# Reordered attention steps in a block-attention and mixture-of-experts kernel

## Chip, cores and metric

The kernel runs on one core of one Trainium2 chip. The metric is device time of one execution, in microseconds (us). Engines are called as the profile calls them: PE (TensorE, matrix products and transposes), PEld (its weight load), DVE (VectorE), ACT (ScalarE), POOL (GpSimd) and SP (SyncE, which issues most DMAs).

## The reference, cut to what matters

Attention runs on 4 batches of 8 heads, 768 positions, 64 columns a head. Each query sees the keys within 15 positions of it, and one maximum over each block of 32 keys; the values that go with the maxima are block means. The rows of the result are then routed to one of 4 groups and one of 4 experts in it, and each token passes through that expert's two matrices.

```python
k_sum = k.reshape(B, H, nb, block, D).max(axis=3)
v_sum = v.reshape(B, H, nb, block, D).mean(axis=3)
scores_l = scale * np.matmul(q, k.transpose(0, 1, 3, 2))      # kept where |i - j| < 16
scores_s = scale * np.einsum('bhsd,bhnd->bhsn', q, k_sum) + np.log(block)
scores_all = np.concatenate([scores_l_m, scores_s], axis=-1)
a = np.exp(scores_all - np.max(scores_all, axis=-1, keepdims=True))
a = a / (np.sum(a, axis=-1, keepdims=True) + 1e-09)
attn_out = np.matmul(a, np.concatenate([v, v_sum], axis=2))
...
h = np.maximum(xg[mask_e] @ w1[g, e], 0.0)
out[tok_idx] = combined[:, None] * (h @ w2[g, e])
```

## The kernel before

**Tiling.** Attention takes two heads at a time: 16 head pairs (`order`, idx 0 to 15), each in three groups (g 0, 1, 2), so 48 groups n = 3·idx + g. A group holds 256 queries of both heads. What follows attention (routing tables, one expert's four blocks, pairs of blocks, single blocks) isn't touched by the change.

**Order of work.** The order in which each engine gets its instructions is written out by hand: `PLAN` (L49) lists the steps of a group for g = 0, 1, 2, and `START` (L52) replaces it for the first groups. The loop at the end of `attention` walks through that list. Every engine works through its own queue in this order, and waits by semaphore for what others make. The steps are:

- s, `scores` (L780): eight score products of 64 by 64 parts of the PE array into two of the three banks `ps_s`; then DVE makes four passes (L795) that add the mask and take a minimum (`ss`, `nm`).
- e, `exps` (L801): four exponentials on ACT (L804) into `pr`.
- t, `transpose_p` (L807): four PE transposes of `pr` of two groups before, into a bank `ps_tr`; ACT copies them to `ptS` (L812).
- v, `values` (L815): eight products of 64 array columns into the one bank `ps_av`, for the group of three before; DVE takes a reciprocal (L826) and multiplies (L827) into `xt`.
- p0, p1 (`put_k`, L760): four transposes of the next pair's keys `kn` for one head each, into `ps_tr`, and two copies (L764) from there into `kw`, j = 0 and j = 1. p2, p3 (`put_q`): the same for the queries, copied by ACT (L758) into `qt`.
- p4 (L769 to L778): on DVE, two copies of neighbouring keys within `kw` (L772, L773), the maxima over 32 keys (L775, `ks`), and their broadcast into the last columns of `kw` (L778). All score products of the next pair read `kw`.
- m0, `means` part 0 (L721): 24 products of 32 array columns with `stair`, and DVE's copy `vp` (L731). m1: two more products, DVE's copy `vr` (L735), and POOL's copies of it into `va` (L738).
- l0, l1 (`logits`): four and two transposes of `xt`, copied to `xT` (L848). l2: eight products of 32 array columns with `wcat`. l3: every fourth pair, two DVE operations (L864, L865) that fill `lg`.

The PE array is thus divided in four ways: whole (all transposes), in 64 by 64 (s), in 64 columns (v), in 32 columns (m0, m1, l2).

**Banks.** `ps_tr` and `ps_s` have three banks each, `ps_av` and `ps_lg` one. `Banks.next` hands them out in turn, so the fourth transpose block waits for the copies of the first.

**Routing.** The tokens' routing is some hundred small DVE operations. `advance(n)` puts the next n of them into DVE's queue at places set by `OPS` (L61): two after v, two within p4 between the maxima and their broadcast, one after the minimum passes of s. Routing work for the three first batches is queued at groups 17, 29 and 41 (`ROUTE_AT`).

**DMAs.** SP issues them in the order of the code. `load_qk` brings keys and queries of a pair (two DMAs of 384 KB), `load_vw` its values in six (L647). The first group of a pair issues values for idx + 2 and then keys and queries for idx + 3. `keep_warm` (L659) puts zero products on PE whose result nobody reads.

Of the kernel before, what the change touches and what calls it, by code (L numbers as in the profile page):

```python
# [20 lines left out]
P = 128  # L21
# [7 lines left out]
NBLK = S // BLOCK  # L29
QT = 64  # L30
RUN = 8
NQT = S // QT

KW = QT + 2 * PAD
NC = KW + NBLK
# [10 lines left out]
EPS = 1e-9  # L46
NEG = -1.0e9

PLAN = [["s", "p0", "l1", "t", "v", "p1", "e", "p4"],  # L49
        ["s", "p2", "t", "v", "m1", "l2", "e"],  # L50
        ["s", "p3", "l3", "t", "v", "l0", "m0", "e"]]
START = [["s", "e"], ["s", "m0", "e"], ["s", "w", "t", "m1", "p0", "p1", "e", "p4", "p2", "p3"],  # L52
         ["t", "v", "s", "n0", "p0", "p1", "e", "p4"]]
LAG = {"l0": 1, "l1": 2, "l2": 2, "l3": 2}

T_LAG, V_LAG = 2, 3
# [1 line left out]
ACT_K1 = range(10, B * NP)  # L58

ROUTE_AT = (17, 29, 41)  # L60
OPS = dict(m=2, k=2, s=(1, 1, 1))  # L61


W1_AT = 34
# [25 lines left out]
class Clock:  # L90

    pe, dve = float("-inf"), 0.0
    step = 0
# [496 lines left out]
def attention(tc, q, k, v, w_group, w_expert, ident, x_dram, ps, router, hook):  # L590
    nc = tc.nc
# [4 lines left out]
    def advance(ops):  # L596

        for _ in range(ops):
            r = next(work[0], work) if work else "wait"
            if r is work:  # L600
                work.pop(0)
            elif r == "wait":
                break
# [6 lines left out]
    V = nc.vector  # L610
    T = router.T
    ps_tr, ps_s, ps_av, ps_lg = ps["tr"], ps["s"], ps["av"], ps["lg"]
    lg = router.lg

    with ExitStack() as st, ExitStack() as nat_st:
# [6 lines left out]
        order = [(b, a) for b in range(B) for a in range(NP)]  # L622
# [16 lines left out]
        def load_vw(idx):  # L639

            b, a = order[idx]
            va = va_ring[idx % NVA][:, :, :, 0:D]
            src = v[b, 2 * a:2 * a + 2]
            for rows, key, t0, t1 in ((slice(0, QT), 0, 0, NQT), (slice(QT, QT + PAD), QT - PAD, 1, NQT),
                                      (slice(QT + PAD, KW), QT, 0, NQT - 1)):
                for h in range(2):
                    nc.sync.dma_start(out=va[rows, t0:t1, h],  # L647
                                      in_=bass.AP(src.tensor, src.offset + (h * S + key) * D,
                                                  [[D, rows.stop - rows.start], [QT * D, t1 - t0], [1, D]]))
# [9 lines left out]
        def keep_warm(n):  # L659
            t = ps_lg.next()  # L660
            for _ in range(n):
                nc.tensor.matmul(out=t, lhsT=zero, rhs=zero[:, None, :].broadcast_to([P, 4, P]), start=True, stop=True)  # L662
# [37 lines left out]
        m = mask[:, 0, 0:KW]  # L700
# [20 lines left out]
        def means(idx, part):  # L721

            va = va_ring[idx % NVA]
            t = ps_tr.next()
            if part == 0:
                for i in range(NQT):
                    j = i % 4
                    T.matmul(out=t[32 * j:32 * j + 32, 0:P], lhsT=stair[:, NBLK - 2 - 2 * i:NBLK + 30 - 2 * i],
                             rhs=va[0:KW, i, :, 0:D], start=(i < 4), stop=(i >= NQT - 4), skip_group_check=True)
                vps[idx] = sm.tile([P, P], F32, name="vp", bufs=2)  # L730
                V.tensor_copy(out=vps[idx], in_=t[:, 0:P])  # L731
            else:
                T.matmul(out=t[KW:NR, 0:P], lhsT=same, rhs=vps.pop(idx), start=True, stop=True)
                vr = wk.tile([NR, 1, 2, D], F32, name="vr")
                V.tensor_copy(out=vr[KW:NR].rearrange("p a h d -> p (a h d)"), in_=t[KW:NR, 0:P])  # L735
                n = 2
                for i in range(0, NQT, n):
                    nc.gpsimd.tensor_copy(out=va[KW:NR, i:i + n, :, 0:D], in_=vr[KW:NR].broadcast_to([NBLK + 1, n, 2, D]))  # L738


        def prep(idx, part):
            qn, kn = qk[idx]
            qb, kw = qts[idx % 2], kws[idx % 2]

            def tr(src, h):

                t = ps_tr.next()
                n = S // RUN
                for i in range(4):
                    T.transpose(out=t[:, i * n:(i + 1) * n], in_=src[:, h, 2 * i:2 * i + 2].rearrange("p j d -> p (j d)"),  # L750
                                identity=ident[0:n, 0:n])
                return [t[64 * j:64 * j + 64, 0:4 * n].rearrange("p (i t r) -> p i t r", i=4, t=NQT) for j in range(2)]

            def put_q(h):
                rows = slice(64 * h, 64 * h + 64)
                out = qb[rows].rearrange("p t (i j) r -> p j t i r", j=2)
                for j, tv in enumerate(tr(qn, h)):
                    nc.scalar.activation(out=out[:, j], in_=tv.rearrange("p i t r -> p t i r"), func=AF.Copy, scale=-1.0 / 8.0)  # L758

            def put_k(h):  # L760
                rows = slice(64 * h, 64 * h + 64)
                out = kw[rows, :, 0:QT].rearrange("p t (r i j) -> p j t r i", i=4, j=2)
                for j, tv in enumerate(tr(kn, h)):
                    (nc.scalar.copy if j == 0 or h and idx in ACT_K1 else V.tensor_copy)(  # L764
                        out=out[:, j], in_=tv.rearrange("p i t r -> p t r i"))
            if part < 2:
                put_k(part)
            elif part < 4:
                put_q(part - 2)  # L769
            else:  # L770

                V.tensor_copy(out=kw[:, 1:NQT, before], in_=kw[:, 0:NQT - 1, QT - PAD:QT])  # L772
                V.tensor_copy(out=kw[:, 0:NQT - 1, behind], in_=kw[:, 1:NQT, 0:PAD])  # L773
                ks = sm.tile([P, NBLK], F32, name="ks")
                V.reduce_max(out=ks, axis=AX.X,  # L775
                             in_=kw[:, :, 0:QT].rearrange("p t (a k) -> p t a k", k=BLOCK))
                advance(OPS["k"])
                V.tensor_copy(out=kw[:, :, KW:NC], in_=ks[:, None, :].broadcast_to([P, NQT, NBLK]))  # L778

        def scores(n):  # L780

# [10 lines left out]
            for h in range(2):  # L792
                for j in range(2):
# [3 lines left out]
                                           accum_out=nm[:, u:u + 1])  # L797
            advance(OPS["s"][g])
            return ss, nm
# [71 lines left out]
        NG = 3 * len(order)  # L871
        prs, pts = {}, {}

        for part in (0, 1, 4, 2, 3):
            prep(0, part)
        keep_warm(9)
        for t in prr:
# [9 lines left out]
        for n in range(NG + 3):  # L887
            idx, g = n // 3, n % 3
            if n < NG:
                b, a = order[idx]  # L890
                xs[b] = x_ring[b % 2]
            for step in START[n] if n < len(START) else PLAN[g]:
                if step == "s" and n < NG:
                    sps = scores(n)
                elif step == "e" and n < NG:
                    prs[n] = exps(n, *sps)
                elif step == "t" and 0 <= n - T_LAG < NG:
                    pts[n - T_LAG] = transpose_p(prs.pop(n - T_LAG))
                elif step == "v" and 0 <= n - V_LAG < NG:
                    values((n - V_LAG) // 3, (n - V_LAG) % 3, pts.pop(n - V_LAG))  # L900
                elif step[0] == "p" and n < NG and idx + 1 < len(order):
                    prep(idx + 1, int(step[1]))
                elif step[0] == "m" and n < NG:
                    j = idx + (step == "m0" and n > 2)
                    if (j > 0 or n < 3) and j < len(order):
                        means(j, int(step[1]))
                elif step == "w":
                    keep_warm(4)
                elif step == "n0":
                    means(1, 0)  # L910
                elif step[0] == "l" and 0 <= idx - LAG[step] < len(order):
                    logits(idx - LAG[step], int(step[1]))
            if n == 0:
                router.consts()
            elif n == 4:
                router.compared()
            if n in ROUTE_AT:
                b1 = ROUTE_AT.index(n)
                work.append(router.route(b1 * TB, (b1 + 1) * TB))
                if b1 == 1:  # L920
                    work.append(router.first_blocks())
            if n == NG - 4:
                nat_st.close()
            if n < NG:
                if g == 0 and idx + 2 < len(order):
                    load_vw(idx + 2)
                if g == 0 and idx < len(order) - 3:
                    qk[idx + 3] = load_qk(idx + 3)
            if g == 1 and stores:
                store()  # L930
            while stores and n == NG - 5:
                store()
            clock.step += 1
            hook(n, need, advance, w1_first)
# [514 lines left out]
```

## Time and profile before

| | us |
|---|---|
| median of 3 runs | 516.33 |
| lowest and highest run | 514.16, 518.73 |
| profiled execution, its time | 515.85 |
| profiled execution, span from first to last instruction | 514.2 |

1.65 us of the profiled execution lie outside its span. Attention runs from the first score products at 9.42 us to about 179 us; the rest belongs to the experts. Times below count from the start of the span. In the timeline a row is a run of like instructions: start, length, engine, line, what it writes and reads, count, and in brackets the idle time before it with what ended it. The length of a PE row includes the pipeline's end, which overlaps the next row, so the step from one start to the next is the measure.

### The profile page before, as it was taken

Reading aid. Unit: us, or ns where it says so; the run is one execution under the profiler, and the core shown is the slowest. Engines: PE = TensorE matmul, PEld = TensorE weight load, DVE = VectorE, ACT = ScalarE, POOL = GpSimd, SP = SyncE. Lnnn points to the kernel's source line nnn. Section 1 sums busy time; section 2 is a strip of 40 time slices with the busy share of each in tenths; the row PEclk is TensorE's granted clock in tenths of the full one; section 3 lists DMA queues with packets and bytes.
Section 4 is the critical chain, followed back from the end, with each engine's and each line's share of the span. In section 5 each row is a group of like instructions: output and inputs, shape, how many; then the busy total and the mean of one; then the engine's idle time right before and its main releaser. Section 6 shows DMA issues by size and latency. Waiting matters only on the chain.

```text
span 514.2 us, 13346 instructions
## 1 busy us (share of the span) xinstructions
PE 492.2 (96%) x4974; PEld 415.5 (81%) x4974; DVE 356.6 (69%) x1084; ACT 317.8 (62%) x597; POOL 120.9 (24%) x205
## 2 busy tenths in 40 slices
PE   8999999999999899999999999999999999999994
PEld 4677767776777698979898989898898989897773
DVE  6687899888977978878755647483836556473773
ACT  5699888888988643216644556473645546474682
POOL 6122112211312600037020203022121202022332
PEclk9799999999999899999999999999999999999998
DMA  9999676879646820069997665665566756754891
GB/s 179 176 181 198 130 168 189 180 155 195 173 113 224 281 90 22 28 220 354 409 403 273 238 229 211 247 225 190 205 211 239 263 212 222 258 191 137 300 359 42
DMA packets 75316, 106.94 MB, mean 208 GB/s; under 512 B 40286, under 2 KB 40366, under 8 KB 75232
## 3 DMA queue, kind: packets, MB, share of 16 engines
q1 hardware_dynamic: 69184, 86.78, 58.5%
q0 software_dynamic: 6048, 19.12, 10.4%
q8 instruction: 43, 0.70, 0.6%
q14 instruction: 41, 0.34, 0.2%
HBM read 97.49 MB, written 13.24 MB: 215 GB/s over the span
## 4 chain that ended last, share of the span: by engine, by line
PE 49%; issue 19%; DMA 12%; DVE 11%; ACT 3%; POOL 3%; POOLq 1%; DVEq 0%; ACTq 0%
PE ps_s L122 26%; DMA out_dram<-y,t_unit_scatter 12%; PE ps_tr L122 12%; PE ps_av L122 10%; DVE ss L795 3%; DVE ks L775 2%; DVE kw L764 1%; ACT kw L764 1%; PE ps_lg L122 1%; POOL ohr L1042 1%; ACT qt L758 1%; PE ps_lg L662 1%; POOLq L1185 1%; ACT pr L804 1%; DVE kw L778 1%
## 5 line engine op out<-in xcount | busy, mean ns | idle before, releaser
L122 DVE TENSOR_TENSOR w2l<-w2r,w2h 128x1024 fp32r<-128x1024 f32 x52 | 63.4, 1225 | 77.1 <-ACT w2h L1035 76.6
L122 PE MATMUL ps_s<-xT,w1h 128*128 128x256 f32 x448 | 83.5, 284 | 0.0
L122 PEld LDWEIGHTS ps_s<-xT,w1h 128*128 128x128 f32 x448 | 70.7, 192 | 1.0 <-issue 0.7
L1082 POOL DMA_INDIRECT out_dram<-y,t_unit_scatter x24 | 25.7, 1069 | 190.9 <-ACT y L1077 97.7
L738 POOL COPY va<-vr 25x256 f32<-25x256 f32 x96 | 35.9, 418 | 118.8 <-DVE vr L735 118.8
L122 PE MATMUL ps_s<-xT,w1l 128*128 128x256 f32 x224 | 63.4, 283 | 0.0
L122 DVE TENSOR_TENSOR w1l<-w1r,w1h 128x1024 fp32r<-128x1024 f32 x52 | 60.4, 1219 | 3.6 <-ACT w1h L1035 3.6
L804 ACT ACTIVATE pr<-ss,nm 128x120 f32<-128x120 f32 x192 | 60.1, 387 | 3.3 <-DVE nm L795 2.9
L1120 ACT ACTIVATE hTh<-ps_s 128x512 fp32r<-128x512 f32 x48 | 28.7, 598 | 53.9 <-PE ps_s L122 31.9
L122 PE MATMUL ps_s<-ohr,w1h 128*128 128x256 f32 x320 | 58.9, 282 | 0.0
L1035 ACT CAST w2h<-w2r 128x1024 fp32r<-128x1024 f32 x52 | 53.8, 1041 | 1.5 <-DVE lg L865 0.9
L1035 ACT CAST w1h<-w1r 128x1024 fp32r<-128x1024 f32 x52 | 50.7, 1051 | 0.4 <-DMA w1r<-in_moe_w_dram 0.4
L122 PEld LDWEIGHTS ps_s<-ohr,w1h 128*128 128x128 f32 x320 | 49.8, 188 | 0.2
L122 DVE SCALAR_TENSOR_TENSOR hTl<-ps_s,hTh 128x512 fp32r<-128x512 f32 x48 | 33.2, 691 | 24.2 <-ACT hTh L1120 21.5
L795 DVE CUSTOM_DVE_ANT_0 ss<-mask,ps_s 128x120 f32<-128x120 f32 x192 | 42.1, 275 | 6.1 <-PE ps_s L122 4.6
L122 PE MATMUL ps_s<-ohr,w1l 128*128 128x256 f32 x160 | 45.0, 281 | 0.0
L122 PEld LDWEIGHTS ps_s<-xT,w1l 128*128 128x128 f32 x224 | 42.9, 192 | 0.3
L122 PE MATMUL ps_s<-kw,qt 64*64 64x120 f32 x768 | 37.5, 282 | 5.7 <-DVE nm L795 4.6
L122 PE MATMUL ps_s<-w2h,hTh 128*128 128x512 f32 x104 | 41.6, 400 | 0.0
L122 PE MATMUL ps_av<-w2h,hTh 128*128 128x512 f32 x104 | 41.6, 400 | 0.0
L122 PE MATMUL ps_av<-w2l,hTh 128*128 128x512 f32 x104 | 41.1, 395 | 0.0
L122 PE MATMUL ps_s<-w2h,hTl 128*128 128x512 f32 x104 | 41.1, 395 | 0.0
(275 smaller groups left out, 1010.6 us busy)
## 6 DMA issues: line engine op xcount, KB each, us to landing
w1r<-in_moe_w_dram SPq DMA_DIRECT2D x30, 1024.0 KB, 8.4
w2r<-in_moe_w_dram SPq DMA_DIRECT2D x28, 1024.0 KB, 5.6
kn<-in_k_dram SPq DMA_DIRECT2D x16, 384.0 KB, 4.5
qn<-in_q_dram SPq DMA_DIRECT2D x16, 384.0 KB, 5.4
va<-in_v_dram SPq DMA_DIRECT2D x32, 192.0 KB, 5.0
x_dram<-xt SPq DMA_DIRECT2D x12, 512.0 KB, 5.4
w2r<-in_moe_w_dram POOLq DMA_DIRECT2D x4, 1024.0 KB
va<-in_v_dram SPq DMA_DIRECT2D x64, 44.0 KB, 4.6
```

The costliest lines, as they stand in the source:

```text
L122: return f(*args, **kw)
L662: nc.tensor.matmul(out=t, lhsT=zero, rhs=zero[:, None, :].broadcast_to([P, 4, P]), start=True, stop=True)
L738: nc.gpsimd.tensor_copy(out=va[KW:NR, i:i + n, :, 0:D], in_=vr[KW:NR].broadcast_to([NBLK + 1, n, 2, D]))
L758: nc.scalar.activation(out=out[:, j], in_=tv.rearrange("p i t r -> p t i r"), func=AF.Copy, scale=-1.0 / 8.0)
L764: (nc.scalar.copy if j == 0 or h and idx in ACT_K1 else V.tensor_copy)(out=out[:, j], in_=tv.rearrange("p i t r -> p t r i"))
L775: V.reduce_max(out=ks, axis=AX.X, in_=kw[:, :, 0:QT].rearrange("p t (a k) -> p t a k", k=BLOCK))
L778: V.tensor_copy(out=kw[:, :, KW:NC], in_=ks[:, None, :].broadcast_to([P, NQT, NBLK]))
L795: V.tensor_tensor_reduce(out=ss[:, u], in0=mask[:, 1 if t == 0 else 2 if t == NQT - 2 else 0], in1=sp[h][:, j], scale=1.0, scalar=3.4e38, ...
L804: nc.scalar.activation(out=pr[:, i, 0:NC], in_=sp[:, i], func=AF.Exp, bias=nm[:, i:i + 1], scale=-1.0)
L1035: self.nc.scalar.copy(out=h, in_=src)
L1082: self.nc.gpsimd.indirect_dma_start(out=self.out, out_offset=bass.IndirectOffsetOnAxis(ap=self.tabs[name, "scatter"][0:y.shape[0], col:col ...
L1120: nc.scalar.activation(out=th[:, js], in_=hp, func=AF.Relu)
```

## The change

The lists of steps are written anew. Products with 32 array columns (m0, l2, m1) now stand together in g = 1, and all full-array transposes of a group stand in one run behind the score products. p4 is split: the copies of neighbours stay p4 and move to g = 1, the maxima and their broadcast become p5 in g = 2. m0 writes a bank of `ps_s` in place of `ps_tr`. Of the key copies, both of the first head go to ACT; of the second head j = 0 goes to ACT from idx 10 on (as `ACT_K1` says), j = 1 to DVE. Routing advances by three behind the broadcast (two between maxima and broadcast before), and not at all behind the minimum passes of g = 2. Values of pair 3 are issued at group 0, right behind those of pair 2, and so ahead of keys and queries of pair 3. The opening gets two and three more zero products (w2, w3) and its lists reach to group 5.

```diff
-PLAN = [["s", "p0", "l1", "t", "v", "p1", "e", "p4"],
-        ["s", "p2", "t", "v", "m1", "l2", "e"],
-        ["s", "p3", "l3", "t", "v", "l0", "m0", "e"]]
-START = [["s", "e"], ["s", "m0", "e"], ["s", "w", "t", "m1", "p0", "p1", "e", "p4", "p2", "p3"],
-         ["t", "v", "s", "n0", "p0", "p1", "e", "p4"]]
+PLAN = [["s", "t", "l1", "p0", "p1", "v", "e"],
+        ["s", "t", "p4", "p2", "v", "m0", "l2", "m1", "e"],
+        ["s", "p5", "t", "p3", "l0", "l3", "v", "e"]]
+START = [["s", "e"], ["s", "m0", "e"], ["s", "w4", "t", "m1", "p0", "p1", "e", "p4", "p5", "p2", "w2", "p3"],
+         ["t", "v", "w3", "s", "n0", "p0", "p1", "e"], ["s", "t", "p4", "p2", "v", "m1", "e"],
+         ["s", "p5", "t", "p3", "v", "l0", "m0", "e"]]
...
-OPS = dict(m=2, k=2, s=(1, 1, 1))
+OPS = dict(m=2, k=3, s=(1, 1, 0))
...
-            t = ps_tr.next()
+            t = (ps_tr if part else ps_s).next()
...
-                    (nc.scalar.copy if j == 0 or h and idx in ACT_K1 else V.tensor_copy)(
+                    (nc.scalar.copy if h == 0 or j == 0 and idx in ACT_K1 else V.tensor_copy)(
...
-            else:
+            elif part == 4:
                 V.tensor_copy(out=kw[:, 1:NQT, before], in_=kw[:, 0:NQT - 1, QT - PAD:QT])
                 V.tensor_copy(out=kw[:, 0:NQT - 1, behind], in_=kw[:, 1:NQT, 0:PAD])
+            else:
                 ks = sm.tile([P, NBLK], F32, name="ks")
                 V.reduce_max(out=ks, axis=AX.X,
                              in_=kw[:, :, 0:QT].rearrange("p t (a k) -> p t a k", k=BLOCK))
+                V.tensor_copy(out=kw[:, :, KW:NC], in_=ks[:, None, :].broadcast_to([P, NQT, NBLK]))
                 advance(OPS["k"])
-                V.tensor_copy(out=kw[:, :, KW:NC], in_=ks[:, None, :].broadcast_to([P, NQT, NBLK]))
...
-        for part in (0, 1, 4, 2, 3):
+        for part in (0, 1, 4, 5, 2, 3):
             prep(0, part)
...
-                elif step == "w":
-                    keep_warm(4)
+                elif step[0] == "w":
+                    keep_warm(int(step[1]))
...
-                if g == 0 and idx + 2 < len(order):
+                if g == 0 and idx != 1 and idx + 2 < len(order):
                     load_vw(idx + 2)
+                    if idx == 0:
+                        load_vw(3)
```

## Rows read from the trace of the kernel before

**Rows 1.** Windows, head pairs 1, 4 and 11, edges at their first score products
```profile
core 0: us, PE busy (x) PEld busy (x) DVE busy (x) ACT busy (x) POOL busy (x), PEclk, DMA share, GB/s
18.70:30.34 11.64, 11.48 (x159) 8.76 (x159) 7.83 (x40) 8.26 (x20) 2.25 (x6) 0.71 1.26 189
...
49.82:59.55 9.73, 9.50 (x168) 7.43 (x164) 8.02 (x39) 8.73 (x23) 2.13 (x6) 1.00 0.66 142
...
121.11:131.76 10.65, 10.15 (x175) 7.77 (x171) 9.13 (x50) 9.32 (x24) 2.61 (x8) 1.00 0.90 184
```

**Rows 2.** Timeline of head pair 4, PE's blocks
```profile
47.82 0.69 PE L122 MATMUL ps_av<-va,ptS 121*64 121x65 f32 x16
...
48.44 0.66 PE L122 MATMUL ps_tr<-ident,xt 128*128 128x128 f32 x4
...
49.02 0.86 PE L122 MATMUL ps_tr<-va,stair 96*32 96x128 f32 x24
...
49.82 0.64 PE L122 MATMUL ps_s<-kw,qt 64*64 64x120 f32 x16
...
50.39 0.55 PE L122 MATMUL ps_tr<-ident,kn 96*128 96x96 f32 x4
...
50.77 0.38 PE L122 MATMUL ps_tr<-ident,xt 128*128 128x128 f32 x2
...
51.00 0.60 PE L122 MATMUL ps_tr<-ident,pr 128*121 128x128 f32 x4
...
55.40 0.42 PE L122 MATMUL ps_s<-kw,qt 64*64 64x120 f32 x2
...
56.62 0.55 PE L122 MATMUL ps_tr<-ident,qn 96*128 96x96 f32 x4
```

**Rows 3.** Timeline of head pair 4, DVE's operations
```profile
50.02 0.29 DVE L731 COPY vp<-ps_tr 128x128 f32<-128x128 f32 x1 [0.83 <-ACT pr L804]
...
50.51 0.28 DVE L795 CUSTOM_DVE_ANT_0 ss<-mask,ps_s 128x120 f32<-128x120 f32 x1 [0.20 <-PE ps_s L122]
...
53.26 0.56 DVE L764 COPY kw<-ps_tr 64x384 f32<-64x384 f32 x1 [0.19 <-ACT kw L764]
...
54.20 0.94 DVE L775 TENSOR_REDUCE ks<-kw 128x24 f32<-128x768 f32 x1
...
55.17 0.31 DVE L778 COPY kw<-ks 128x288 f32<-128x288 f32 x1
...
55.51 0.28 DVE L795 CUSTOM_DVE_ANT_0 ss<-mask,ps_s 128x120 f32<-128x120 f32 x1
...
56.31 0.18 DVE L826 RECIPROCAL rs<-ps_av 128x4 f32<-128x4 f32 x1
```

**Rows 4.** DVE's waits, 69.30 to 164.05 us: total us, times, longest
```profile
DVE kw L772 <- ACT kw L764: 2.6, 6, 0.7
DVE vp L731 <- ACT xT L848: 2.2, 3, 1.1
DVE rs L826 <- PE ps_av L122: 1.9, 4, 1.1
...
DVE vp L731 <- ACT pr L804: 1.2, 2, 0.8
```

**Rows 5.** Costliest groups of the page: the exponentials on ACT
```profile
L804 ACT ACTIVATE pr<-ss,nm 128x120 f32<-128x120 f32 x192 | 60.1, 387 | 3.3 <-DVE nm L795 2.9
```

**Rows 6.** Timeline of the opening: zero products, DMA issues on SP, key transposes
```profile
12.69 1.04 PE L662 MATMUL ps_lg<-zero 128*128 128x512 bf16 x4
...
22.51 0.38 SPq L633 DMA_DIRECT2D kn<-in_k_dram  x1
...
23.74 5.85 SPq L647 DMA_DIRECT2D va<-in_v_dram  x6
...
30.91 0.55 PE L122 MATMUL ps_tr<-ident,kn 96*128 96x96 f32 x4
```

**Rows 7.** DMA issues of the page: count, KB, median us to landing
```profile
kn<-in_k_dram SPq DMA_DIRECT2D x16, 384.0 KB, 4.5
```

## The prediction, made before the changed kernel ran

> **What bounds the kernel now.** I read the page first: PE is busy nearly all the span, which for pipelined products says little. So I cut attention, the only part that the change touches, into windows by head pair [rows 1]. Pair 4 takes 9.73 us, with PE busy 9.50, ACT 8.73, DVE 8.02, at full granted clock; pairs 2 to 5 are alike. Pair 11 stands for pairs 6 to 14, where routing work is under way: 10.65 us, DVE busy 9.13 although one key copy of it has gone to ACT. The nine pairs from 69.30 to 164.05 us take 94.75 us, 10.53 each. Pair 1, in the opening, takes 11.64 us at a mean granted clock of 0.71, that is partly at 1.2 in place of 2.4 GHz; against 9.73 this is 1.9 us.
>
> Next the timeline of pair 4 [rows 2], start to start. Score products take 0.57 us (49.82 to 50.39). The score products at 55.40 take 1.22 until the next block at 56.62, 0.65 more. DVE's rows [rows 3] say why: it goes from the key copy (53.26) through the maxima (54.20) and the broadcast (55.17) to the minimum passes at 55.51 without a pause, and the second score bank is free only when the passes of the group before are done. So in pairs 2 to 5 PE sets the pace, with one stall of 0.65 us behind DVE.
>
> DVE itself waits in every pair [rows 3]: 0.83 us ahead of the copy vp, 0.20 ahead of the minimum passes, 0.19 ahead of a key copy. The wait of vp is labelled with ACT, but what vp reads is the block of 24 products that PE began at 49.02 [rows 2]. From 69.30 to 164.05 us [rows 4] DVE waits 2.6 us for ACT ahead of L772, 2.2 + 1.2 ahead of vp, 1.9 for the value products: 7.9 of 94.75 us. With routing in its queue DVE is close to being the bound there, and its waits are what can be gained.
>
> **The change, part by part.**
>
> *Fewer changes of array division.* Counting through the lists, a pair before goes whole, 64 by 64, whole, 64 columns and so on in 13 changes; after, in 10. What one costs: four transposes between two changes take 0.58 us (48.44 to 49.02), two in the middle of a run 0.23 (50.77 to 51.00), so four would take 0.46; the difference, 0.12, is what a run pays for its changes [rows 2]. Bounds are 0, where PE waits anyway, and 0.2. Three fewer are 0.36 us of PE time a pair. Here a rule of the Trainium skill speaks against the gain: the page TensorEngine Tiling (Array Packing), section PSUM Bottleneck, says in substance that packing speeds up PE but not the emptying of PSUM, which may then become the bound, and advises to use both ScalarE and VectorE for it. By that rule alone the 0.36 would be worth nothing. The traces bear it out in part: ACT and DVE, which empty the banks, are busy 8.73 and 8.02 of 9.73 us [rows 1], so little room is left below 9 us. It is the third of the cases below.
>
> *p4 split and moved, routing behind the broadcast.* DVE now does neighbours in g = 1 and maxima and broadcast in g = 2, behind that group's minimum passes. The stall of 0.65 goes, since between two groups' minimum passes there is never more than one of these. What comes in its place: the next pair's score products need the broadcast, made in the group just before them. From the start of g = 2's score products: 0.69 until DVE's first pass (49.82 to 50.51), 0.80 for four passes (55.51 to 56.31), 0.97 for the maxima (54.20 to 55.17), 0.34 for the broadcast (to 55.51): 2.80 us [rows 2, 3]. PE's own work in g = 2 is 0.57 for scores, 0.46 for t, 0.38 for p3 (as 50.39 to 50.77), 0.58 for l0, 0.62 for v (47.82 to 48.44): 2.61 [rows 2]. So PE waits 0.2 us a pair if DVE is not late, and one for one more if it is. Moving advance behind the broadcast takes two operations out of this path; the count of routing operations a pair stays 11 (six behind v, three, two).
>
> *Full-array run t, l1, p0, p1.* p1 is the fourth block in three banks, so it waits for the copy ptS of t. That copy stands in ACT's queue behind the exponentials of the group before, four of 387 ns [rows 5]. The wait is between 0 and 1.5 us; I take 0.4, since PE has scores, t, l1 and p0 to do first.
>
> *Key copies by head.* The count on each engine stays two and two (three and one from idx 10). Now no half is split over both, except from idx 10 on. Before, DVE's copy started only when ACT's was done [rows 3], and p4 right behind it waited for ACT [rows 4]; after, p4 runs a group later, when these copies are old. m0's bank from ps_s lets its products go without waiting for a transposed bank, but it takes score banks: g = 2's scores now need all minimum passes of g = 1. PE has 3 us of work in between, so I set this at nothing; if DVE is later than that, it is part of the fourth case.
>
> So pairs 2 to 5: 0.36 + 0.65 gained, 0.2 + 0.4 lost, 0.4 each, 1.6 us together (9.3 a pair). Pairs 6 to 14: DVE's list is as long as before, so only its waits count. Those for ACT and for m0, 6.0 us, lose their cause; I give back 1.2 for new ones: 4.8 us. Bounds are 0 and the whole 7.9.
>
> *Fourth values sooner.* On SP, keys and queries of pair 3 go behind six more DMAs. Before, keys were issued at 22.51 and those six took 5.85 us of SP (from 23.74) [rows 6]. After, keys leave at about 28.4 and, with the median landing of 4.5 us [rows 7], arrive by 32.9. The transposes that need them began at 30.91 [rows 6]. So p0 of group 6 can be up to 2.0 us late; what follows it in its group is shorter than before by t and l1, 0.5 + 0.2 us [rows 2]. That is a loss of up to 1.3 us, or of nothing if the keys come 2 us sooner than their median.
>
> *Zero products.* Five more, 0.26 us each by 12.69's row [rows 6], 1.3 us, stand where PE waits for ACT and DVE in the opening and are hidden; uncovered they cost that. They may keep the clock at 2.4 GHz through pair 1, worth up to 1.9 us. But whatever pair 1 gains, p0 of group 6 then waits for its keys. So I set the opening at 0, from 1.9 gained to 2.6 lost. Such a wait can itself bring the clock down a little later.
>
> *End of attention and experts.* Pair 15 prepares no next pair, and the experts' code is the same: 0.
>
> Sum: 515.85 - 1.6 - 4.8 = 509.45 for an execution like the profiled one. This was 0.48 below the median of 516.33, so I predict 509.9.
>
> **The rivals.**
>
> *All engines reach their floors.* Pairs 2 to 5 fall to PE's 9.73 - 0.65 - 0.36 = 8.7 (4.0 us), all of DVE's 7.9 go, and the opening keeps the 1.9: 515.85 - 13.8 + 0.48 = 502.5. For it: DVE's floor in pair 4 is 9.73 - 1.22 = 8.5. Against: three engines would have to be full at once.
>
> *Emptying sets the pace.* DVE and ACT have the same work to do, and while routing runs nothing is gained: only the 1.6 of pairs 2 to 5 stays, 515.85 - 1.6 + 0.48 = 514.7. The rule of the Trainium skill named above would have it so. For it: the same instructions on both; against: the waits in [rows 4] are of order, not of work.
>
> *The broadcast comes too late: slower.* While routing runs, six operations of a pair's 11 lie on DVE between g = 0's start and g = 2's minimum passes. Pair 11's DVE is 1.1 us busier than pair 4's, and with the 0.56 of the copy that left, routing is 1.7 us a pair [rows 1, 3]; six of eleven are 0.9. If DVE reaches the passes of g = 2 that much late, PE waits 0.2 + 0.9 + 0.4 where it saved 1.0: 0.5 lost a pair, 4.5 in nine, less 1.6: 515.85 + 2.9 + 0.48 = 519.2; with all 1.7 late, 526. It decides from a lateness of 0.4. For it: s is at the head of every group. Against: in these pairs DVE, not PE, is nearly the bound, and a PE wait is then free.
>
> **How the numbers follow.** Forecast 0.52, floors 0.13, emptying 0.23, broadcast 0.12. The forecast's own range is 506.5 to 513, by the bounds of its 4.8 and of the opening. Leaving out half of the floors' case below and most of the last above, the range is 503.5 to 519. One per cent, about what a measurement of this kernel can tell from no change, is 5.2 us: faster means under 511.2, slower over 521.5. Three quarters of the forecast and all of the floors' case are faster, 0.52; the last case's upper half and some opening trouble are slower, 0.09; the rest, 0.39, is the same.
>
> **What would show it.** Pairs 2 to 5 at 9.2 to 9.4 us; score products at the head of a pair waiting 0.2 to 0.4 us for the broadcast; the waits of key copies and L772 for ACT gone from DVE's list; DVE busy over 9.3 of some 10.0 us in pairs 6 to 14; a PE wait of 1 to 3 us for kn at group 6, near 29 to 32 us. I'd be wrong if pairs 6 to 14 stay at 10.5 (emptying, or the broadcast), if PE's wait for the broadcast is over 1 us, or if the opening moves by more than 2 us.

## The result and the profile after

| | before | after |
|---|---|---|
| median, us (13 runs each, beside each other) | 515.80 | 520.96 |
| lowest and highest run, us | 513.86, 518.95 | 516.45, 522.52 |
| ratio of after to before, 95% interval | | 1.0089 [1.0068, 1.0111] |
| profiled execution: its time, span, us | 515.85, 514.2 | 517.72, 516.0 |

The changed kernel is slower by 0.9%, 4.6 us by the ratio, where 6.4 us less were forecast, and lies beyond the top of the range. The profiled execution of it is one of its three quickest, so its trace shows less of the loss than the median: 1.9 us.

From the page of the changed kernel, its span, busy times and granted clock in 40 slices:

```profile
span 516.0 us, 13360 instructions
...
PE 483.7 (94%) x4979; PEld 413.1 (80%) x4979; DVE 353.9 (69%) x1084; ACT 314.9 (61%) x597; POOL 120.5 (23%) x205
...
PEclk9999999999999999999999999999999999999998
```

This execution ran attention at full clock throughout, where the one before had 1.2 GHz in part of pair 1 [rows 1]. Up to the first score products of pair 15 the two are level, 164.09 us after and 164.05 before, with some 1.3 us of before's spent at the lower clock in pair 1 (b0, below). The 1.8 us between their spans lie behind that, where the code is the same: 0.3 up to the experts' first product, 0.5 up to PE's last, 1.0 behind it. So the loss of the medians can't be read from this one pair of traces; what they do show is where the forecast gains went. Windows of the changed kernel by head pair (1, 2, 4, then 6 to 14, then 11), columns as in [rows 1]:

```profile
18.97:27.89 8.92, 8.64 (x160) 6.62 (x159) 7.22 (x39) 7.13 (x18) 2.26 (x6) 1.00 1.08 162
27.89:40.23 12.34, 9.49 (x168) 7.72 (x164) 7.86 (x39) 9.18 (x24) 2.14 (x6) 1.00 1.12 210
49.76:59.58 9.82, 9.12 (x164) 7.47 (x164) 7.75 (x40) 8.42 (x23) 2.14 (x6) 1.00 0.81 140
69.39:164.09 94.70, 83.63 (x1505) 68.17 (x1505) 80.79 (x427) 82.34 (x215) 19.26 (x54) 1.00 0.78 179
120.67:131.40 10.73, 9.35 (x172) 7.61 (x172) 8.57 (x50) 8.82 (x24) 2.14 (x6) 1.00 0.85 179
```

Against [rows 1]: pair 1 went from 11.64 to 8.92 us, pair 4 from 9.73 to 9.82, pairs 6 to 14 from 94.75 to 94.70, pair 11 from 10.65 to 10.73. Pair 2, 9.73 before, takes 12.34. In pair 4 PE is busy 0.38 us less than before and the pair is longer: PE's work did shrink, and waiting took its place. In pairs 6 to 14 PE is busy 5.1 us less (88.72 to 83.63), DVE the same (81.20 to 80.79), and nothing came of it. By the starts of score products the nine pairs fall in two parts: pairs 6 to 8 take 30.75 us for 31.66 before, pairs 9 to 14 take 63.95 for 63.09. What the first three gained, 0.9, the last six lost.

**Where pair 4 waits.** Timeline of the changed kernel, pair 4, answering to [rows 2] and [rows 3]:

```profile
49.76 0.70 PE L123 MATMUL ps_s<-kw,qt 64*64 64x120 f32 x16 [0.29 <-DVE kw L779]
...
51.14 0.49 PE L123 MATMUL ps_tr<-ident,kn 96*128 96x96 f32 x4
...
51.43 0.57 ACT L814 COPY ptS<-ps_tr 121x512 f32<-121x512 f32 x1
...
52.05 0.36 PEld L123 LDWEIGHTS ps_tr<-ident,kn 96*128 96x128 f32 x4 [0.60 <-ACT ptS L814]
52.05 0.55 PE L123 MATMUL ps_tr<-ident,kn 96*128 96x96 f32 x4 [0.42 <-ACT ptS L814]
...
52.71 1.13 DVE L765 COPY kw<-ps_tr 64x384 f32<-64x384 f32 x2 [0.87 <-PE ps_tr L123]
...
58.00 0.59 ACT L814 COPY ptS<-ps_tr 121x512 f32<-121x512 f32 x1 [0.94 <-PE ps_tr L123]
...
58.61 0.69 PE L123 MATMUL ps_av<-va,ptS 121*64 121x65 f32 x16
```

The reader is to see two stalls of PE. p1 (52.05) can't start until ACT has emptied t's bank into `ptS`; PE's weight loads stand idle 0.60 us for it, PE 0.42, and DVE then waits 0.87 for the second head's transposes. And the score products at the head of a pair wait for the broadcast (49.76); from 58.61, where v begins, to the next pair's score products at 59.58 it is 0.97 us, where v alone took 0.62 [rows 2]. That is 0.35. ACT is late with `ptS` at one end of the pair and itself waits 0.94 for PE at the other (58.00): a loop, not an engine that is full.

**Where pairs 6 to 14 wait.** Waits from 69.39 to 164.09 us in the changed kernel: us in total, times, longest; first DVE's, then PE's:

```profile
DVE kw L765 <- ACT kw L765: 7.8, 6, 1.9
...
PE ps_s L123 <- DVE kw L779: 4.8, 8, 1.0
```

The waits of [rows 4] are gone, and one new line of DVE's, 7.8 us, is as long as all of them together (7.9). All of it lies behind 100.14 us, where the keys of idx 10 and later are prepared and the second head's two copies are split: j = 0 on ACT, j = 1 on DVE, and DVE's follows ACT's, which is the third of three copies in a row on ACT.

**The opening.** Timeline of the changed kernel, PE and SP, answering to [rows 6]:

```profile
14.72 12.57 SPq L648 DMA_DIRECT2D va<-in_v_dram  x12
27.39 0.38 SPq L634 DMA_DIRECT2D kn<-in_k_dram  x1
...
29.27 0.38 PE L123 MATMUL ps_tr<-ident,xt 128*128 128x128 f32 x2
31.93 0.85 PE L123 MATMUL ps_tr<-ident,kn 96*128 96x96 f32 x8 [2.27 <-DMA kn<-in_k_dram]
```

Keys of pair 3 left SP at 27.39 in place of 22.51, and PE waited 2.27 us for them in pair 2.

### The profile page after: what moved, and what is told of

Read it like the earlier page. It is cut to its first block, busy times and chain, and to the rows that moved or that the text cites. A ratio compares the mean times of both kernels' runs of the same rounds, so it can differ in the third digit from the quotient of the medians.

```text
span 516.0 us, 13360 instructions
## 1 busy us (share of the span) xinstructions
PE 483.7 (94%) x4979; PEld 413.1 (80%) x4979; DVE 353.9 (69%) x1084; ACT 314.9 (61%) x597; POOL 120.5 (23%) x205
## 5 line engine op out<-in xcount | busy, mean ns | idle before, releaser
L1086 POOL DMA_INDIRECT out_dram<-y,t_unit_scatter x24 | 27.0, 1126 | 190.0 <-ACT y L1081 97.6
L739 POOL COPY va<-vr 25x256 f32<-25x256 f32 x96 | 34.4, 403 | 118.7 <-DVE vr L736 109.2
L123 PE MATMUL ps_s<-w2l,hTh 128*128 128x512 f32 x104 | 41.1, 395 | 0.0
```

The source lines that it names most:

```text
L123: return f(*args, **kw)
L1086: self.nc.gpsimd.indirect_dma_start(out=self.out, out_offset=bass.IndirectOffsetOnAxis(ap=self.tabs[name, "scatter"][0:y.shape[0], col:col ...
```

## Experiments

One table for all runs, read from the starts of score products in each trace: time from the first of all score products to the first of pair 3 (the opening), the length of pair 4, and that of pairs 6 to 14; in us.

| run | opening | pair 4 | pairs 6 to 14 | profiled execution |
|---|---|---|---|---|
| before | 30.65 | 9.73 | 94.75 | 515.85 |
| before again (b0) | 29.30 | 9.73 | 94.76 | 514.66 |
| after | 30.81 | 9.82 | 94.70 | 517.72 |
| after again (a1) | 29.72 | 9.81 | 94.61 | 519.10 |
| a2 values late | 29.81 | 9.81 | 94.60 | 517.53 |
| a3 copies | 34.02 | 9.82 | 91.27 | 520.29 |
| a4 maxima early | 30.86 | 9.82 | 95.85 | 520.79 |
| a5 p1 behind v | 30.14 | 9.33 | 90.51 | 516.38 |
| a6 m0 back | 31.41 | 9.30 | 92.76 | 515.16 |
| a7 no zeros | 31.78 | 9.81 | 94.61 | 517.49 |
| b1 values alone | 32.72 | 9.73 | 94.75 | 517.47 |
| c1 = a2 + a5 | 30.36 | 9.33 | 90.51 | 511.67 |
| c2 = a2 + a5 + a6 | 27.89 | 9.05 | 89.40 | 508.43 |

The two columns on the right of the opening repeat to 0.1 us between runs of like code; the opening does not. So each stage is judged by its own column, and the opening by the medians as well.

**a1: the changed kernel again**, for runs beside those of a2 to a4.

> The changed kernel, unaltered, for the spread of its runs and a second trace. Theory C (clock and late keys): the wait for the keys of pair 3 in group 6, 2.27 us in the first trace, lowers the granted clock soon after in most runs; runs with mean clock 0.994 or more take 516 to 518 us, runs near 0.985 take 521 to 522.5, and a trace with the lower clock has a stretch at 1.2 GHz between 30 and 45 us. Theory W (waits moved) expects pairs 3 to 5 near 9.8 us in any trace, and the difference between runs elsewhere than in the opening.

520.71 us against 517.58 for before, ratio 1.0079 [1.0047, 1.0110]. The loss holds.

**a2: fourth values at their old place.**

```diff
-                if g == 0 and idx != 1 and idx + 2 < len(order):
+                if g == 0 and idx + 2 < len(order):
                     load_vw(idx + 2)
-                    if idx == 0:
-                        load_vw(3)
```

> Values of pair 3 issued at group 3 again, behind keys and queries of pair 3. Theory C: the wait for keys in group 6 (2.27 us) goes, means of pair 3 may wait about 1 us for their values, the clock no longer falls there, and the time is 3 to 5 us lower than the changed kernel's. Theory W: the opening gains at most 1 to 2 us and the pairs from 3 on stay at 9.5 to 9.8 us.

517.84 us, ratio to before 1.0010 [0.9988, 1.0032], where the changed kernel had 1.0079 beside it. This edit alone takes away the loss, some 3.6 us by the ratios and 2.9 by the medians; pair 4 and pairs 6 to 14 don't move. The values have their own deadline, though: m0 stands in g = 1 since the change, and PE waits 0.49 us for them in a2's pair 2 and 1.39 in that of c1 below. In c2, with m0 back in g = 2, there is no such wait. From the windows of a2, pair 2:

```profile
28.71:39.42 10.71, 9.52 (x168) 7.74 (x165) 7.91 (x40) 8.63 (x23) 2.13 (x6) 1.00 1.30 180
```

**b1: the fourth values sooner in the kernel before, nothing else** (the same lines, the other way round).

> The kernel before with the values of pair 3 sent at group 0, alone. Theory C: p0 of group 6 waits for its keys 1 to 2 us, a fall of the clock near 32 us follows in a part of the runs, and the time is 1 to 3 us above the kernel before. If the order of these DMAs doesn't matter: the same time within 0.5 us.

517.98 us, ratio 1.0075 [1.0043, 1.0107]. This is the mirror of a2: one edit to the kernel before makes nearly the whole loss (3.9 us by the ratio, 2.9 by the medians). Timeline of b1's PE, and its windows of pairs 1 and 2:

```profile
31.76 0.52 PE L122 MATMUL ps_tr<-ident,kn 96*128 96x96 f32 x4 [1.92 <-DMA kn<-in_k_dram]
```
```profile
18.70:29.20 10.50, 9.09 (x159) 6.78 (x159) 7.79 (x40) 8.24 (x20) 2.21 (x6) 1.00 1.15 173
29.20:42.13 12.93, 11.01 (x169) 8.65 (x165) 8.11 (x39) 8.72 (x23) 2.17 (x7) 0.87 1.10 213
```

The same wait of PE for the same keys, and behind it a granted clock of 0.87 over pair 2: part of that pair ran at 1.2 GHz. Pair 2 took 12.93 us, 3.2 more than before's 9.73.

**a3: from idx 10 on the first head's copies are split, not the second's.**

```diff
-(nc.scalar.copy if h == 0 or j == 0 and idx in ACT_K1 else V.tensor_copy)(
+(nc.scalar.copy if (h == 1 or j == 0 if idx in ACT_K1 else h == 0) else V.tensor_copy)(
```

(Three copies stay on ACT from idx 10 on, but DVE's one is now of the first head, whose transposes are p0's and early.)

> From pair 10 on, the key copies go as before (first head: ACT and DVE, second head: both ACT); earlier pairs as in the change. Theory W: DVE's wait for ACT ahead of its key copy, 7.8 us in 6 waits in pairs 6 to 14, falls to under 2 us, and these pairs lose 3 to 5 us in sum. If DVE's list of work alone sets the pace there, the wait turns into another one and the sum of these pairs stays within 1 us.

517.71 us, ratio 1.0014 [0.9985, 1.0042]. Windows of a3, pair 2 and pairs 9 to 14; DVE's largest wait from 100.70 to 164.63 us; and PE's timeline in pair 2:

```profile
29.21:43.92 14.71, 11.62 (x167) 9.53 (x164) 7.77 (x39) 8.11 (x21) 2.13 (x6) 0.77 0.99 203
104.06:164.63 60.57, 56.12 (x1005) 45.73 (x1005) 51.34 (x281) 56.73 (x147) 12.79 (x36) 1.00 0.74 181
```
```profile
DVE kw L765 <- ACT kw L765: 2.4, 4, 0.8
```
```profile
33.50 1.51 PE L123 MATMUL ps_tr<-ident,kn 96*128 96x96 f32 x8 [2.80 <-DMA kn<-in_k_dram]
```

Pairs 9 to 14 take 60.57 us where the changed kernel took 63.95 (100.14 to 164.09): 3.4 less, with DVE's wait for ACT's copy down from 7.8 to 2.4 (under 2 was expected). The trace also holds the dearest opening of all: a wait of 2.80 us for the keys, and pair 2 at 14.71 us with a granted clock of 0.77.

**a4: maxima and broadcast a group earlier.**

```diff
-        ["s", "t", "p4", "p2", "v", "m0", "l2", "m1", "e"],
-        ["s", "p5", "t", "p3", "l0", "l3", "v", "e"]]
+        ["s", "t", "p4", "p5", "p2", "v", "m0", "l2", "m1", "e"],
+        ["s", "t", "p3", "l0", "l3", "v", "e"]]
```

(and the last two lists of `START` alike.)

> Maxima and broadcast (p5) in g = 1 behind p4, a group earlier. Theory W: PE's wait for the broadcast at the head of a pair (0.3 to 0.4 us in pairs 3 to 5, 4.8 us of PE in pairs 6 to 14) goes; pairs 3 to 5 fall from 9.8 to about 9.4, and the time by 3 to 4 us. If the place doesn't matter, the same time comes back as a wait of g = 2's scores for the minimum passes of g = 1.

520.74 us, ratio 1.0046 [1.0019, 1.0073]: neither of the two expectations. The wait for the broadcast is gone from pair 4, and pair 4 is 9.82 us as before. Timeline of a4 at the head of pair 5:

```profile
60.76 0.98 ACT L759 ACTIVATE qt<-ps_tr 64x384 f32<-64x384 f32 x2
...
61.79 0.41 PEld L123 LDWEIGHTS ps_s<-kw,qt 64*64 64x64 f32 x14 [0.23 <-ACT qt L759]
```

Score products now begin at 61.37 and wait in their middle for ACT's query copies, which come in ACT's queue behind `ptS`. Freed of one wait, the loop through ACT closes by another path at the same length. Pairs 6 to 14 grow from 94.70 to 95.85 us, so making the broadcast sooner gained nothing there.

**a5: p1 behind v.**

```diff
-PLAN = [["s", "t", "l1", "p0", "p1", "v", "e"],
+PLAN = [["s", "t", "l1", "p0", "v", "p1", "e"],
```

> The key transposes p1 behind v again, two array changes more. Theory L (a loop through ACT: scores and t of g = 2 on PE, then on ACT ptS, the query copies, xT, the exponentials and the next ptS, then p1, v and all of g = 1 on PE) says that p1's wait for ptS, 0.6 us a pair, holds pairs 3 to 5 at 9.8; with v in between it goes, for about 0.15 of array changes: 9.3 to 9.5 us a pair. If DVE's or ACT's list of work alone sets the pace: 9.8 and more.

One run, 516.38 us, beside a median of 516.22 for before, with the fourth values still sooner. (c1, below, has the same edit in ten runs.) Windows of a5, pair 4 and pairs 6 to 14; then DVE's wait for ACT's copy in the latter:

```profile
50.55:59.88 9.33, 9.04 (x164) 7.46 (x164) 7.75 (x40) 8.40 (x23) 2.13 (x6) 1.00 0.82 148
69.22:159.73 90.51, 83.55 (x1504) 68.18 (x1504) 80.57 (x427) 82.28 (x215) 19.18 (x54) 1.00 0.77 183
```
```profile
DVE kw L765 <- ACT kw L765: 0.4, 1, 0.4
```

v's products (0.62 us) now stand between p0 and p1 and cover ACT's `ptS`; by the lists this is one array change more, not two. Pair 4 falls by 0.49 us, pairs 6 to 14 by 4.2 (all of it in pairs 9 to 14: 59.75 us for 63.95), and DVE's 7.8 us of waiting become 0.4, though the copies stay split as the change has them. Pair 10 shows what did it; first the changed kernel, whose pair begins at 109.90, then a5, whose pair begins at 109.27:

```profile
112.04 1.56 ACT L765 COPY kw<-ps_tr 64x384 f32<-64x384 f32 x3
112.19 0.55 PE L123 MATMUL ps_tr<-ident,kn 96*128 96x96 f32 x4 [0.41 <-ACT ptS L814]
113.64 0.56 DVE L765 COPY kw<-ps_tr 64x384 f32<-64x384 f32 x1 [1.38 <-ACT kw L765]
114.23 0.18 DVE L828 RECIPROCAL rs<-ps_av 128x4 f32<-128x4 f32 x1
```
```profile
111.40 1.56 ACT L765 COPY kw<-ps_tr 64x384 f32<-64x384 f32 x3
111.69 0.55 PE L123 MATMUL ps_tr<-ident,kn 96*128 96x96 f32 x4
111.80 0.18 DVE L828 RECIPROCAL rs<-ps_av 128x4 f32<-128x4 f32 x1 [0.18 <-PE ps_av L123]
112.02 0.42 DVE L829 TENSOR_TENSOR xt<-ps_av,rs 128x256 f32<-128x256 f32 x1
112.99 0.57 DVE L765 COPY kw<-ps_tr 64x384 f32<-64x384 f32 x1
```

From the start of the pair, p1 comes at 2.29 us and in a5 at 2.42, ACT's three copies end at 3.70 and 3.69, and DVE's copy starts at 3.74 and 3.72. So p1 is no sooner in a5, nor is the copy. What differs is DVE's queue: in a5 v's reciprocal and multiplication, and two routing operations after them, stand ahead of the copy and fill the time in which DVE stood idle for ACT; in the changed kernel they stood behind it.

**a6: m0 back in g = 2.**

```diff
-        ["s", "t", "p4", "p2", "v", "m0", "l2", "m1", "e"],
-        ["s", "p5", "t", "p3", "l0", "l3", "v", "e"]]
+        ["s", "t", "p4", "p2", "v", "l2", "m1", "e"],
+        ["s", "p5", "t", "p3", "l0", "l3", "v", "m0", "e"]]
```

> m0 at the end of g = 2, as before the change; one array change more. Theory L: PE's 0.7 us for m0 leave g = 1 and so the loop through ACT: pairs 3 to 5 at 9.1 to 9.3 in place of 9.8, and PE no longer waits for the broadcast. If the lists of ACT and DVE set the pace: 9.8. Pairs 6 to 14 lose less, since DVE's wait for ACT ahead of its key copy (7.8 us) stays.

516.02 us, ratio 0.9994 [0.9963, 1.0024]. Timeline of a6's PE in pair 4:

```profile
52.13 0.36 PEld L123 LDWEIGHTS ps_tr<-ident,kn 96*128 96x128 f32 x4 [0.36 <-ACT ptS L814]
...
58.64 0.86 PE L123 MATMUL ps_s<-va,stair 96*32 96x128 f32 x24
59.44 0.64 PE L123 MATMUL ps_s<-kw,qt 64*64 64x120 f32 x16
```

By the starts of the three groups, pair 4 is 3.39 + 3.49 + 2.95 us in the changed kernel and 3.09 + 2.83 + 3.38 here. Taking m0 out of g = 1 saves 0.66; putting it into g = 2 costs only 0.43, since it fills the time in which PE waited for the broadcast (58.64 to 59.44, with no wait ahead of the score products); and p1 waits 0.36 in place of 0.60, most of the 0.30 by which g = 0 is shorter.

**a7: no added zero products** in the opening (no "w2" and "w3" in `START`).

> Without the five added zero products. If they hold the clock up in pair 1, a stretch at 1.2 GHz near 19 us comes back as in the kernel before, pair 1 takes 11 to 12 us in place of 9, the wait for the keys in group 6 shrinks by as much, and the time stays within 1.5 us or gets better, since group 6 then has no long wait that lowers the clock. If they do nothing: the same trace as the changed kernel's.

518.78 us, ratio 1.0062 [1.0033, 1.0091]: no different from the changed kernel's 1.0089 and 1.0079, whose intervals overlap it. Pair 1 took 9.23 us at full clock without them, so they are not what made pair 1 short. Windows of a7 within pair 2: up to the keys' landing, just behind it, and the rest:

```profile
28.18:31.50 3.32, 1.76 (x26) 1.27 (x22) 1.85 (x11) 2.43 (x7) 0.00 (x0) 1.00 0.92 227
31.50:35.70 4.20, 3.83 (x43) 3.21 (x44) 1.96 (x7) 2.14 (x6) 0.00 (x0) 0.59 1.08 233
35.70:41.20 5.50, 5.26 (x102) 4.29 (x100) 4.29 (x25) 4.14 (x10) 2.13 (x6) 1.00 1.26 180
```

PE was busy 1.76 of 3.32 us, waiting for the keys, and then ran at a granted clock of 0.59, mostly 1.2 GHz, for four microseconds.

**b0: the kernel before again.**

> The kernel before, unaltered, for a second trace. Pairs 2 to 5 at 9.74 us, pairs 6 to 14 at 94.7 us in sum; the opening's stretch at 1.2 GHz near 19 us again, if it belongs to the kernel and not to one execution. The stretch behind the last PE work, 6.8 us in the first trace and 7.4 to 9.6 in those since, within 7 to 10 us if that is spread between executions.

514.66 us, at full clock all through attention: pair 1 took 10.30 us in place of 11.64 [rows 1]. So 1.3 us of pair 1 in the first trace of before was the clock, and not something that every execution has.

**c1 and c2: what the findings give together.** c1 is a2 and a5; c2 is a2, a5 and a6.

> Two parts of the change undone: p1 behind v again, values of pair 3 at group 3 again. Theory L gives pairs 3 to 14 5.4 us less than either kernel (118.5 us in the run with p1 behind v alone, 123.9 in both kernels); with no wait for keys in group 6 the opening is no worse than before. So 510 to 513 us, 4 to 6 below the kernel before. If what pairs 3 to 14 gain comes back at the end of attention, 515 to 517.

> As the one before, and m0 at the end of g = 2 as before the change. Theory L: both edits take their part out of the same loop, so pairs 3 to 5 go from 9.33 to 9.0 to 9.2, with less of PE's wait for the broadcast, and the time is 0 to 3 us below the run with p1 and values alone. If ACT's and DVE's lists set the pace from 9.3 on: the same time.

c1 512.20 us, ratio 0.9944 [0.9923, 0.9965]; c2 508.82 us, ratio 0.9888 [0.9846, 0.9931]: c2 is quicker than both kernels, and 3.4 us quicker than c1 by the medians, where 0 to 3 were expected. Windows of c2, pairs 2 and 4 and pairs 6 to 14:

```profile
28.17:37.43 9.26, 9.26 (x168) 7.53 (x165) 8.05 (x40) 8.97 (x24) 2.13 (x6) 1.00 1.29 181
46.48:55.53 9.05, 9.05 (x168) 7.34 (x164) 7.92 (x40) 8.52 (x23) 2.13 (x6) 1.00 1.11 169
64.59:153.99 89.40, 84.94 (x1508) 67.67 (x1504) 81.21 (x427) 82.25 (x214) 19.17 (x54) 1.00 0.80 189
```

PE is busy all of pairs 2 and 4. Here PE's own work sets the pace, which was the aim; in the changed kernel it did not.

## Why the prediction was wrong, point by point

Forecast were 1.6 us less in pairs 2 to 5, 4.8 less in pairs 6 to 14 and 0 in the opening, 6.4 less in all. Measured: 0.1 more a pair (9.82 for 9.73 in pair 4), nothing in pairs 6 to 14, and some 3.6 to 3.9 more for the fourth values by a2's and b1's ratios (2.9 by the medians). The first was a sum of terms a little off; the other two are the failed steps.

**"Full-array run t, l1, p0, p1 ... I take 0.4."** The mechanism was named rightly, p1 as the fourth block in three banks, waiting for ACT's `ptS`. Its size in pair 4 was 0.53: p1 stands 0.91 us behind p0 (51.14 to 52.05), where four such transposes took 0.38 [rows 2]; a5 gives 0.49 net, with an array change coming back. What failed was to look at PE alone. With p1 ahead of v in the list, p1's copies stand ahead of v's work in DVE's queue as well: DVE stood idle 0.87 us for p1's transposes in pair 4, and in pairs 9 to 14, where its copy follows ACT's third, 7.8 us.

**"Those for ACT and for m0, 6.0 us, lose their cause; I give back 1.2 for new ones."** The waits of [rows 4] did lose their cause, but 7.8 us came in their place. The prediction did note that from idx 10 on a half is split over both engines, and put no price on it. Two runs show the cause from two sides: a3 gives DVE a copy of p0's bank, which follows the first of ACT's three (3.4 us less); a5 leaves the copies as they are and puts v's work ahead of DVE's (4.2 us less). With a5 the term is nearly what was forecast, 4.2 for 4.8.

**"So I set the opening at 0, from 1.9 gained to 2.6 lost."** All its parts were seen: keys issued at 27.39 (28.4 expected), PE's wait of 2.27 us (between 1 and 3 expected), and, in a3, a4, a6, a7 and b1, a lower clock behind it, which the prediction named and gave no price. But they were set against a gain of clock in pair 1 that isn't the change's: pair 1 ran at full clock in b0 and in a7 too. (Pair 1 did get shorter at full clock, 10.30 in b0 to 8.92, and 9.23 without the zero products, so by the new order of its steps.) And the wait was to cost up to 1.3; pair 2 cost 2.6 us without a fall (12.34 for 9.73) and 5.0 with the longest (14.71 in a3). a2 and b1 both show this edit as the loss. The traces' openings differ less than the medians: 31.4 us on average over the eight traces with early fourth values, 29.6 over the five without. Of those eight, the five with a fall of the clock in pair 2 have 32.2, the three others 30.2. Both traces of the changed kernel itself are without a fall there, at mean granted clocks of 0.996 and 0.995, and its executions differ: of the 13, three had 0.994 to 0.997 and took 516.45 to 517.72 us, ten had 0.984 to 0.988 and took 519.36 to 522.52. That most of them pay a fall in pair 2, which the traces then miss, would fit, but isn't shown: the kernel before has executions at low clocks as well (0.979 to 0.993 in the 25 beside a1), and its own trace and six more have a stretch at 1.2 GHz near the end of attention. So the cause of the loss is shown, and its size in the traces only in part; the first score products, too, start anywhere between 9.41 and 11.13 us in like kernels.

**The small terms of pairs 2 to 5.** *Stall of 0.65*: gone, as said. *Array changes, 0.36*: what is left of pair 4 without its waits is 9.82 - 0.53 - 0.35 = 8.94, against 9.73 - 0.65 = 9.08 before, so 0.14. Between them lie a5, with 11 changes (9.33 less 0.36 of waiting for the broadcast: 8.97), and c2, with 12 (9.05). By this estimate, which takes all else as equal, a change costs some 0.05 us, not 0.12. *Broadcast, 0.2*: 0.35. *m0's bank, "I set this at nothing"*: a6 and c2 keep the bank, so it isn't that. But m0's products, taken from g = 2, would have covered the wait for the broadcast; a6 shows 0.5 us a pair for moving them back, part of it p1's. Stall, changes, p1 and broadcast make a gain of 0.65 + 0.14 - 0.53 - 0.35 = -0.09, as measured (the changes being what the others leave), where +0.4 was forecast.

**End of attention and experts, 0.** From pair 15 to the first product of the experts it is 15.92 us after and 15.60 before. Behind the last product on PE the two profiled executions differ by 0.96 us (7.81 and 6.85), which is spread: 6.5 to 9.6 over all traces, with the same code there.

**The rivals.** *All engines reach their floors* did not happen: the best version's pair 4 is 9.05, not 8.7. *The broadcast comes too late* did happen as a wait: 4.8 us of PE's time in pairs 6 to 14. But it was not the loss, since with the broadcast made a group earlier (a4) those pairs took longer, not less, and a5 has 4.9 us of it and is 4.2 us shorter. *Emptying sets the pace* gives the right picture of pairs 6 to 14, no gain, for a wrong reason: a5 and c2 do the same emptying, with ACT busy 82.28 and 82.25 us and DVE 80.57 and 81.21, in 90.51 and 89.40 us in place of 94.70. The waits were of order, as the prediction had it against this rival.

The rule of the Trainium skill behind that rival, TensorEngine Tiling (Array Packing), section PSUM Bottleneck, says that where tiling speeds up TensorE, emptying PSUM may become the bound, and advises to share it between ScalarE and VectorE. The traces agree that PE's saving can be worth nothing (5.1 us less of busy PE in pairs 6 to 14, and no gain), but not that the work of emptying is why. And its advice has a limit here: the 7.8 us of DVE waiting for ACT stood between two copies out of one bank that both engines shared. Whether the bank ties them or `kw`, which both write, no run here separates.

## What to carry to other kernels

A step that needs the result of another engine's queue belongs behind work that covers it: grouping instructions to save a change of array division (some 0.05 us each here) cost 0.5 us a pair where it put the fourth user of three banks directly behind the first three. In a schedule that goes round through several engines, price a wait by who waits for the waiting instruction, down to the copies and the engine after it, and read what each engine's queue holds behind the waiting one: work that doesn't need the late result can go ahead of it, as in a5. Then look for what is late next in the same loop, as a4 did. Before a transfer is sent sooner, follow the one that it is put ahead of: six small transfers moved up here made a larger one, with a nearer deadline, late.

## What the runs showed of the chip that was not expected

PE's granted clock fell behind a wait in pair 2 in five traces (a3, a4, a6, a7, b1), and not in three others (after, a1, a5). In a3 it was 0.77 over pair 2, in b1 0.87, in a7 0.59 over the four microseconds behind the keys' landing. Before each fall PE had stood waiting for the keys (2.80 us in a3, 2.04 in a6, 1.92 in a7 and b1, 1.67 in a4). After shorter waits it kept 2.4 GHz (1.21 in a1, 1.04 in a5), but in the changed kernel's own trace it waited 2.27 us and kept it too. So the length of the wait alone doesn't say whether an execution will pay for it, and a single profile, as the one of after, can miss the price.
